# Seven block products in place of eight in the second feed-forward product, with the operand sums on VectorE and GpSimd

## The chip, the cores and the metric

The kernel runs on one core of a Trainium2 chip. The metric is the device time of one launch in microseconds (us): 325.04 us before the change, median of three runs (324.2 to 325.07). All times of "before" below are of runs on the same chip in the same rounds as the kernel they are set against.

## The reference, cut to what matters

Windowed attention (each query sees keys at most 32 positions away), then a two-layer feed-forward block with a tanh gelu between the layers. All inputs are float32.

```python
def reference(q, k, v, w_in, w_out):          # q, k, v: [8, 8, 576, 64]
    s = q @ k.transpose(0, 1, 3, 2) / 8       # only |i - j| <= 32 kept
    attn = softmax(s) @ v
    x = attn.transpose(0, 2, 1, 3).reshape(4608, 512)
    h = x @ w_in                              # w_in  [512, 2048]
    g = 0.5 * h * (1 + tanh(c * (h + 0.044715 * h**3)))
    return g @ w_out                          # w_out [2048, 512]
```

## The kernel before

The 4608 rows are worked in nine tiles of 512 (0 to 8). In each tile TensorE does the first product (16 groups of four 512-column matmuls, each group followed by a gelu on ScalarE), then the second product. The attention of the batch that the next tile needs is woven into the second product. While the first product runs, VectorE casts q and k of that batch to float16, and a DMA transposes them.

```python
PLAN = {3: ([-1], [0]), 14: ([], [1]), 24: ([0], [2]), 35: ([1], [3]), 46: ([2], [4]), 58: ([3], [])}

    def cast_and_turn(b):
        # ... buffers ...
        for src, dst in ((qr, q16), (qt, qt16)):
            for pr in range(NPAIR):
                nc.vector.tensor_copy(...)                 # 4 casts of q, 4 of its tail
            nc.sync.dma_start_transpose(...)
        for pr in range(NPAIR):
            nc.vector.tensor_copy(k16[:, pr, :, :, :], kr[:, :, 2 * pr:2 * pr + 2, :])
            nc.sync.dma_start_transpose(...)               # 4 of k; then its tail

    def ffn_in(t, fc, d0=0, d1=4):
        # ... bank ph; gTs[t] is one single buffer for all tiles ...
        for dc in range(d0, d1):
            nc.tensor.matmul(ph, w_in16[...], xT[...], start=(dc == 0), stop=(dc == 3))
        if d1 == 4:
            nc.scalar.activation(gTs[t][:, fc, :], ph, AF.Gelu_apprx_tanh)

    def ffn_out(t, t4, fc):
        # ... four row blocks t4 of 128, sixteen matmuls of 512 columns each ...
            nc.tensor.matmul(py[:, cols], gTs[t][:, f, t4 * 128:t4 * 128 + 128],
                             w_out16[:, f, cols], start=(f == 0), stop=(f == NF - 1))
        if f == NF - 1:
            yo = yp.tile([128, 512], FP32, name="yo", tag="yo")      # yp has 3 buffers
            # ... copy out of PSUM, store row block t4 at once ...
```

The softmax here doesn't subtract the row's maximum and nothing guards it: scores larger than these inputs give would overflow.

## Time and profile before

| | before |
|---|---|
| time, median | 324.63 us (in the rounds of the change) |
| span of the profiled run | 323.7 us |
| first matmul of tile 1 / 2 / 3 / 7 / 8 | 62.54 / 96.15 / 129.75 / 264.18 / 292.44 us |
| end of the last matmul | 320.12 us |

The chain that ended last, in order of time, gives the period of a tile; its columns are start, length, engine, tile, line and how many instructions. Each line is the start of a first product.

```profile
96.15 0.65 PE mm L439 x3
...
129.75 0.65 PE mm L439 x3
...
163.36 0.65 PE mm L439 x3
```

The period is 33.60 us.

### The profile page before, as it was taken

Reading aid. Unit: us, or ns where it says so; the run is one execution under the profiler, and the core shown is the slowest. Engines: PE = TensorE matmul, PEld = TensorE weight load, DVE = VectorE, ACT = ScalarE, POOL = GpSimd, SP = SyncE. Lnnn points to the kernel's source line nnn. Section 1 sums busy time; section 2 is a strip of 40 time slices with the busy share of each in tenths; the row PEclk is TensorE's granted clock in tenths of the full one; section 3 lists DMA queues with packets and bytes.
Section 4 is the critical chain, followed back from the end, with each engine's and each line's share of the span. In section 5 each row is a group of like instructions: output and inputs, shape, how many; then the busy total and the mean of one; then the engine's idle time right before and its main releaser. Section 6 shows DMA issues by size and latency. Waiting matters only on the chain.

```text
span 323.7 us, 5827 instructions
## 1 busy us (share of the span) xinstructions
PE 311.7 (96%) x2265; PEld 153.4 (47%) x2265; DVE 136.0 (42%) x290; ACT 201.8 (62%) x316; POOL 59.5 (18%) x82
## 2 busy tenths in 40 slices
PE   7688999999999999999999999999999999999995
PEld 2463545444554445444544454445444544444444
DVE  5655587641556064705570467034713530110011
ACT  1757577578667766777577766777668577705600
POOL 3646356292031101300040104010000000000000
PEclk9959999999999999999999999999999999999999
DMA  7999998999989596949495979799270220031022
GB/s 208 259 362 362 381 277 230 251 161 157 248 155 160 95 245 159 169 88 251 115 155 116 221 161 135 134 203 183 75 122 17 67 58 9 0 91 41 0 60 70
DMA packets 120490, 50.57 MB, mean 156 GB/s; under 512 B 100784, under 2 KB 112048, under 8 KB 120464
## 3 DMA queue, kind: packets, MB, share of 16 engines
q1 hardware_dynamic: 88752, 45.07, 58.2%
q0 software_dynamic: 31520, 4.98, 21.0%
q8 instruction: 17, 0.28, 0.4%
q10 hardware_dynamic: 192, 0.16, 0.2%
q14 instruction: 9, 0.07, 0.1%
HBM read 37.62 MB, written 9.44 MB: 145 GB/s over the span
## 4 chain that ended last, share of the span: by engine, by line
PE 93%; SPq 2%; DMA 2%; DVE 1%; ACT 0%; issue 0%; POOL 0%; POOLq 0%
PE mm L461 39%; PE mm L439 24%; PE ph L439 14%; PE ps_o L381 5%; PE ps_s L348 5%; PE ps_d L381 4%; DMA vr<-in_v_dram 2%; SPq L126 1%; PE py L461 1%; ACT gT L443 0%; SPq L135 0%; PE pt L277 0%; DVE w_out L186 0%; PE pt L279 0%; DVE KT L285 0%
## 5 line engine op out<-in xcount | busy, mean ns | idle before, releaser
L461 PE MATMUL mm<-w_out,gT 128*128 128x512 f16 (+1 forms) x576 | 132.0, 377 | 0.8 <-DVE w_out L186 0.8
L439 PE MATMUL mm<-xT,w_in 128*128 128x512 f16 x360 | 89.0, 382 | 0.0
L439 PEld LDWEIGHTS <-w_in 128*128 128x128 f16 x576 | 56.2, 98 | 68.6 <-DVE w_in L186 1.5
L461 PEld LDWEIGHTS <-gT 128*128 128x128 f16 x592 | 54.2, 98 | 61.8 <-issue 0.6
L443 ACT ACTIVATE gT<-mm 128x512 f16<-128x512 f32 x90 | 53.7, 597 | 35.5 <-PE mm L439 35.5
L439 PE MATMUL ph<-xT,w_in 128*128 128x512 f16 x216 | 57.3, 381 | 1.2 <-ACT gT L443 1.2
L354 ACT ACTIVATE pe<-ps_s 128x704 f16<-128x704 f32 x64 | 43.3, 727 | 9.9 <-PE ps_s L348 9.2
L395 ACT ACTIVATE lt<-ps_d 128x480 f32<-128x480 f32 (+3 forms) x40 | 22.2, 555 | 43.2 <-PE ps_d L381 43.1
L443 ACT ACTIVATE gT<-ph 128x512 f16<-128x512 f32 x54 | 32.2, 597 | 13.3 <-PE ph L439 13.3
L405 DVE TENSOR_TENSOR xT<-ps_o,lt 128x480 f16<-128x480 f32 (+5 forms) x38 | 20.3, 552 | 46.9 <-ACT lt L396 46.8
L411 DVE TENSOR_TENSOR xT<-ps_o,lt 128x384 f16<-128x384 f32 (+1 forms) x8 | 4.3, 541 | 80.7 <-ACT lt L396 80.7
L363 DVE TENSOR_TENSOR pe<-pe,mask 128x704 f16<-128x704 f16 x64 | 34.4, 543 | 6.3 <-ACT pe L354 4.0
L465 DVE COPY yo<-mm 128x512 f32<-128x512 f32 x35 | 23.9, 685 | 31.1 <-PE mm L461 28.4
L166 POOL DMA_DIRECT2D V<-in_v_dram x24 | 23.8, 1005 | 63.6 <-PE ps_o L381 47.4
L381 PEld LDWEIGHTS <-V 128*64 128x64 f16 x336 | 18.9, 114 | 18.1 <-issue 11.9
L381 PE MATMUL ps_o<-pe,V 128*64 128x160 f16 (+2 forms) x244 | 22.8, 249 | 1.6 <-POOL V L258 1.5
L396 ACT ACTIVATE lt<-lt 128x480 f32<-128x480 f32 (+3 forms) x40 | 23.5, 588 | 1.3
L381 PE MATMUL ps_d<-pe,ones 128*64 128x192 f16 (+2 forms) x264 | 23.8, 246 | 0.0
L348 PE MATMUL ps_s<-QT,KT 64*128 64x192 f16 (+5 forms) x336 | 19.1, 230 | 2.2 <-DVE KT L285 2.2
L381 PEld LDWEIGHTS <-ones 128*64 128x64 f16 x336 | 19.5, 115 | 0.0
L348 PEld LDWEIGHTS <-KT 64*128 64x128 f16 x336 | 10.9, 95 | 10.6 <-issue 4.2
L168 POOL DMA_DIRECT2D V<-in_v_dram x6 | 5.3, 878 | 56.3 <-PE ps_d L381 39.2
(56 smaller groups left out, 154.3 us busy)
## 6 DMA issues: line engine op xcount, KB each, us to landing
kr<-in_k_dram SPq DMA_DIRECT2D x32, 256.0 KB
qr<-in_q_dram SPq DMA_DIRECT2D x6, 1024.0 KB
V<-in_v_dram POOLq DMA_DIRECT2D x30, 128.0 KB, 5.6
wst<-in_moe_w_in_dram SPq DMA_DIRECT2D x3, 1024.0 KB
wst<-in_moe_w_out_dram SPq DMA_DIRECT2D x3, 1024.0 KB
qr<-in_q_dram SPq DMA_DIRECT2D x8, 256.0 KB
vr<-in_v_dram SPq DMA_DIRECT2D x16, 128.0 KB
out_dram<-yo SPq DMA_DIRECT2D x30, 48.0 KB
```

Source lines behind the costliest of these rows:

```text
L166: nc.gpsimd.dma_start(V[:, c, :, :], v[b, :, 128 * c:128 * c + 128, :].rearrange("h p d -> p h d"))
L348: nc.tensor.matmul(ps[:, h, off:off + 4 * n].rearrange("k (j p) -> k j p", j=4), KTs[b % 2][r0:r0 + 64, pr, k0:k0 + 128], QTs[b][r0:r0 + 6 ...
L354: nc.scalar.activation(pe, ps[:, :, 0:w], AF.Exp, scale=SCALE)
L363: nc.vector.tensor_tensor(pe, pe, m.rearrange("p (o w) -> p o w", o=1).broadcast_to(list(pe.shape)), op=ALU.mult)
L381: nc.tensor.matmul(bk[r0:r0 + 64, at:at + 4 * n].rearrange("d (j p) -> d j p", j=4)[:, :, p0 - q0:p1 - q0], V[:, c, 2 * pr + h, :] if w == ...
L395: nc.scalar.activation(lt[:, 0:n], d[:, 0:n], AF.Ln)
L396: nc.scalar.activation(lt[:, 0:n], lt[:, 0:n], AF.Exp, scale=-1.0)
L405: nc.vector.tensor_tensor(xT[:, g, pos:pos + e], o[:, done:done + e], lt[:, done:done + e], op=ALU.mult)
L439: nc.tensor.matmul(ph, w_in16[:, dc, fc * 128:fc * 128 + 128], xT[:, dc, t * 512 % RING:t * 512 % RING + 512], start=(dc == 0), stop=(dc = ...
L443: nc.scalar.activation(gTs[t][:, fc, :], ph, AF.Gelu_apprx_tanh)
L461: nc.tensor.matmul(py[:, cols], gTs[t][:, f, t4 * 128:t4 * 128 + 128], w_out16[:, f, cols], start=(f == 0), stop=(f == NF - 1))
L465: (nc.scalar.copy if last and half == 0 else nc.vector.tensor_copy)(yo[:, cols], py[:, cols])
```

## The change

The second product of tiles 1 to 8 is cut into 2 by 2 blocks and done with seven block products instead of eight, by sums of blocks made beforehand (the scheme known as Winograd's form of Strassen's). T1 to T4 are sums of weight blocks, made once, at the end of tile 0. S1 to S4 are sums of gelu blocks, made in every tile, a quarter at a time after every fourth gelu; the groups of the first product are taken in another order, so that each quarter has its blocks together. The products of a pair are accumulated in PSUM (the memory that this kernel's matmuls write their results to, in pieces called banks) where the scheme allows it; VectorE adds the rest when it empties a bank. TensorE's share should shrink by an eighth. The price is work on VectorE and GpSimd, and outputs that are finished later.

```diff
+WINO = [("A11", "B11", True), ("S2", "T2", True), ("A12", "B21", False), ("S3", "T3", False),
+        ("S1", "T1", True), ("A22", "T4", False), ("S4", "B22", False)]
+PLAN = {6: "s0 v-1", 24: "s1", 26: "m0", 32: "x-1", 40: "m1", ...}
-    yp = ctx.enter_context(tc.tile_pool(name="yp", bufs=3))
+    yp = ctx.enter_context(tc.tile_pool(name="yp", bufs=2))
 ...
     def ffn_in(t, n, d0=0, d1=4):
 ...
             nc.scalar.activation(gTs[t][:, fc, :], ph, AF.Gelu_apprx_tanh)
+            if t and n % 4 == 3:
+                sums(t, n // 4)
+    def combine_w():
+        for eng, dst, x, y in ((nc.vector, T1, B12, B11), (nc.vector, T2, B22, T1),
+                               (nc.gpsimd, T3, B22, B12), (nc.gpsimd, T4, B21, T2)):
+            eng.tensor_tensor(dst, x, y, op=ALU.subtract)
+    def sums(t, i):
+        third = nc.vector if t == 1 else nc.gpsimd
+        for eng, dst, x, y, op in ((nc.vector, S1, A21, A22, ALU.add),
+                                   (nc.vector, S2, S1, A11, ALU.subtract),
+                                   (third, S3, A11, A21, ALU.subtract),
+                                   (nc.gpsimd, S4, A12, S2, ALU.subtract)):
+            eng.tensor_tensor(dst, x, y, op=op)
 ...
+    def ffn_out(t, i):                       # 7 products of 16 matmuls of 256 columns
+        n, blk, f = i // 16, i // 8 % 2, i % 8
 ...
+        elif n == 5:
+            nc.vector.tensor_tensor(C21, py, M1, op=ALU.add)
+            for x in range(2):
+                store(t, 2 + x, yo[:, 2 + x, :])
+                if end:                      # last tile
+                    store(t, x, yo[:, x, :], left)
+    def ffn_last(t):
+        for x in range(2):
+            nc.vector.tensor_tensor(yo[:, x, right], py[:, x, :], yo[:, x, right], op=ALU.add)
+            store(t, x, yo[:, x, :], right if t == NT - 1 else slice(0, 512))
 ...
         if t == 0:
             load_v(2)
+            combine_w()
```

Tile 0 keeps its eight products. Its output copies share the buffers `yp`, now two.

More of the change, by code (lines that the diff above doesn't have):

```diff
@@ L35, in width @@
     return sum(4 * (p1 - p0) for (_, _, p0, p1) in pieces)
-PLAN = {3: ([-1], [0]), 14: ([], [1]), 24: ([0], [2]), 35: ([1], [3]), 46: ([2], [4]), 58: ([3], [])}
+WINO = [("A11", "B11", True), ("S2", "T2", True), ("A12", "B21", False), ("S3", "T3", False),
+        ("S1", "T1", True), ("A22", "T4", False), ("S4", "B22", False)]
+PLAN = {6: "s0 v-1", 24: "s1", 26: "m0", 32: "x-1", 40: "m1", 42: "v0 s2", 48: "x0", 56: "m2",
+        61: "v1 s3", 64: "x1", 80: "m3", 81: "v2 s4", 88: "x2", 97: "v3", 104: "m4", 112: "x3"}
 TURN_0 = {9: 0, 11: 1, 13: 2, 15: 3}
@@ L49 @@
            [(t4, fc) for t4 in (2, 3) for fc in range(16)])
-END = (3, 0, 2, 1)
 RING = 1536
@@ L413, in spread, with ffn_in @@
                 lt[:, 0:n].rearrange("d (r q) -> d r q", r=NPAIR), op=ALU.mult)
-    def values(b, g):
-        o, d = weigh(b, g)
-        spread(b, g, o, invert(b, g, d))
     gTs = {}
     phs = {}
-    def ffn_in(t, fc, d0=0, d1=4):
-        if fc == 0 and d0 == 0:
+    def ffn_in(t, n, d0=0, d1=4):
+        fc = n // 2 + 8 * (n % 2) if t else n
+        if n == 0 and d0 == 0:
             gTs[t] = gp.tile([128, NF, 512], FP16, name="gT", tag="gT")
@@ L432, in ffn_in @@
                 if t:
-                    i = (0, 2, 1)[fc % 3] if fc < NF - 1 else 2
+                    i = (first(t), 2, 1 - first(t))[n % 3] if n < NF - 1 else 2
                 else:
@@ L443, in ffn_in, with first @@
             nc.scalar.activation(gTs[t][:, fc, :], ph, AF.Gelu_apprx_tanh)
+            if t and n % 4 == 3:
+                sums(t, n // 4)
+    def first(t):
+        return (t + 1) % 2
+    wino = {}
+    def combine_w():
+        t12 = stage.tile([128, 2, 8, 256], FP16, name="t12", tag="stage")
+        t34 = stage.tile([128, 2, 8, 256], FP16, name="t34", tag="stage")
+        B11, B12, B21, B22 = (w_out16[:, r:r + 8, c:c + 256] for r in (0, 8) for c in (0, 256))
+        T1, T2, T3, T4 = t12[:, 0], t12[:, 1], t34[:, 0], t34[:, 1]
+        for eng, dst, x, y in ((nc.vector, T1, B12, B11), (nc.vector, T2, B22, T1),
+                               (nc.gpsimd, T3, B22, B12), (nc.gpsimd, T4, B21, T2)):
+            eng.tensor_tensor(dst, x, y, op=ALU.subtract)
+        s12 = stage.tile([128, 2, 8, 256], FP16, name="s12", tag="stage")
+        s34 = stage.tile([128, 2, 8, 256], FP16, name="s34", tag="stage")
+        yo = stage.tile([128, 4, 512], FP32, name="y4", tag="stage")
+        wino.update(B11=B11, B21=B21, B22=B22, T1=T1, T2=T2, T3=T3, T4=T4, S1=s12[:, 0],
+                    S2=s12[:, 1], S3=s34[:, 0], S4=s34[:, 1], yo=yo)
@@ new lines, in sums @@
+    def sums(t, i):
+        g, r = gTs[t], slice(2 * i, 2 * i + 2)
+        A11, A21, A12, A22 = (g[:, r0 + 2 * i:r0 + 2 * i + 2, c:c + 256]
+                              for r0 in (0, 8) for c in (0, 256))
+        S1, S2, S3, S4 = (wino[f"S{n}"][:, r, :] for n in (1, 2, 3, 4))
+        third = nc.vector if t == 1 else nc.gpsimd
[4 more added lines that the diff above has]
+            eng.tensor_tensor(dst, x, y, op=op)
@@ L445 @@
     out_v = out.rearrange("(b p j) f -> b j p f", b=B, j=4)
     pys = {}
-    def ffn_out(t, t4, fc):
-        last = t == NT - 1 and t4 == END[-1]
-        if last:
-            half, fc = divmod(2 * fc, NF)
-            halves = [slice(256 * half, 256 * half + 256)] * 2
-        else:
-            half, halves = 0, [slice(0, 512)]
-        for f, cols in enumerate(halves, fc):
-            if f == 0:
-                pys[t4] = bank((END.index(t4) if t == NT - 1 else t4) % 2) if half == 0 else \
-                    psO.tile([128, 512], FP32, name="py2", tag="O")
-            py = pys[t4]
-            nc.tensor.matmul(py[:, cols], gTs[t][:, f, t4 * 128:t4 * 128 + 128],
-                             w_out16[:, f, cols], start=(f == 0), stop=(f == NF - 1))
-        if f == NF - 1:
-            yo = yp.tile([128, 512], FP32, name="yo", tag="yo")
-            (nc.scalar.copy if last and half == 0 else nc.vector.tensor_copy)(
-                yo[:, cols], py[:, cols])
-            m = 0
-            while m < 128:
-                b, c = divmod(t * 512 + t4 * 128 + m, S)
-                q0, n = (0, cut(b)) if c < 4 * cut(b) else (cut(b), 144 - cut(b))
-                j, p = divmod(c - 4 * q0, n)
-                e = min(n - p, 128 - m)
-                eng = nc.scalar if last and m else nc.sync if t else nc.gpsimd
-                eng.dma_start(out_v[b, j, q0 + p:q0 + p + e, cols], yo[m:m + e, cols])
-                m += e
@@ new lines, in store, with ffn_out_0 @@
+    def store(t, t4, yo, cols=slice(0, 512), eng=None):
+        m = 0
+        while m < 128:
+            b, c = divmod(t * 512 + t4 * 128 + m, S)
+            q0, n = (0, cut(b)) if c < 4 * cut(b) else (cut(b), 144 - cut(b))
+            j, p = divmod(c - 4 * q0, n)
+            e = min(n - p, 128 - m)
+            (eng or nc.sync).dma_start(out_v[b, j, q0 + p:q0 + p + e, cols], yo[m:m + e, cols])
+            m += e
+    def ffn_out_0(t4, fc):
+        if fc == 0:
+            pys[t4] = bank(t4 % 2)
+        nc.tensor.matmul(pys[t4], gTs[0][:, fc, t4 * 128:t4 * 128 + 128], w_out16[:, fc, :],
+                         start=(fc == 0), stop=(fc == NF - 1))
+        if fc == NF - 1:
+            yo = yp.tile([128, 512], FP32, name="yo", tag="yo")
+            nc.vector.tensor_copy(yo, pys[t4])
+            store(0, t4, yo, eng=nc.gpsimd)
@@ new lines, in ffn_out @@
+    def ffn_out(t, i):
+        n, blk, f = i // 16, i // 8 % 2, i % 8
+        a, w, new = WINO[n]
+        if i % 16 == 0 and new:
+            pys[n % 2] = bank((first(t) + n) % 2)
+        py = pys[n % 2].rearrange("p (b c) -> p b c", b=2)
+        if a[0] == "A":
+            r0, c0 = 8 * (int(a[2]) - 1) + f, 256 * (int(a[1]) - 1) + 128 * blk
+            lhsT = gTs[t][:, r0, c0:c0 + 128]
+        else:
+            lhsT = wino[a][:, f, 128 * blk:128 * blk + 128]
+        nc.tensor.matmul(py[:, blk, :], lhsT, wino[w][:, f, :], start=(new and i % 16 == 0),
+                         stop=(i % 16 == 15), skip_group_check=True)
+        if i % 16 < 15:
+            return
+        yo, left, right = wino["yo"], slice(0, 256), slice(256, 512)
+        C11, C12, C21, C22 = (yo[:, r:r + 2, c] for r in (0, 2) for c in (left, right))
+        end = t == NT - 1
+        M1, U2, U3 = C21, C12, C22
+        if n == 0:
+            nc.vector.tensor_copy(M1, py)
+        elif n == 1:
+            nc.vector.tensor_tensor(U2, py, M1, op=ALU.add)
+        elif n == 2:
+            nc.vector.tensor_copy(C11, py)
+        elif n == 3:
+            nc.vector.tensor_tensor(U3, py, M1, op=ALU.add)
+        elif n == 4:
+            nc.vector.tensor_tensor(C22, py, U3, op=ALU.add)
+        elif n == 5:
[4 more added lines that the diff above has]
+                    store(t, x, yo[:, x, :], left)
@@ L478 @@
+    def ffn_last(t):
+        py = pys[0].rearrange("p (b c) -> p b c", b=2)
+        yo, right = wino["yo"], slice(256, 512)
+        for x in range(2):
+            nc.vector.tensor_tensor(yo[:, x, right], py[:, x, :], yo[:, x, right], op=ALU.add)
+            store(t, x, yo[:, x, :], right if t == NT - 1 else slice(0, 512))
     cast_open(0)
@@ L588 @@
                 ffn_in(t, fc)
-        plan = PLAN if att else {3: ([-1], [])} if t == B - 1 else {}
+        plan = PLAN_0 if not t else PLAN if att else {6: "v-1", 32: "x-1"} if t == B - 1 else {}
         def group(g):
@@ L597 @@
             load_qk(b + 1)
-        if t == 0:
-            ods = {}
-        for i in range(64):
-            for act in PLAN_0.get(i, "").split() if t == 0 else ():
+        ods = {}
+        for i in range(113 if t else 65):
+            for act in plan.get(i, "").split():
                 kind, g = act[0], int(act[1:])
@@ L623 @@
                     ods[g] = (o, invert(bb, gg, d))
+                    if t and g < 0 and b + 1 < B:
+                        load_v(b + 1)
                 else:
                     spread(*group(g), *ods[g])
-            if t and i in plan:
-                for g in plan[i][0]:
-                    values(*group(g))
-                    if g < 0 and b + 1 < B:
-                        load_v(b + 1)
-                for g in plan[i][1]:
-                    score(*group(g))
-                    mask(*group(g))
-            if t:
-                ffn_out(t, END[i // NF] if t == NT - 1 else i // NF, i % NF)
-            else:
-                ffn_out(t, *ORDER_0[i])
+            if t == 0 and i < 64:
+                ffn_out_0(*ORDER_0[i])
+            elif t and i < 112:
+                ffn_out(t, i)
         if t == 0:
             load_v(2)
+            combine_w()
+        else:
+            ffn_last(t)
         begun = 2 if att else 0
```

## The prediction

> **What bounds the kernel now.** I read the page's busy shares first, then the chain that ended last, then the groups by shape, then the timeline at the places where the change puts new waits. The page:
>
> ```profile
> PE 311.7 (96%) x2265; PEld 153.4 (47%) x2265; DVE 136.0 (42%) x290; ACT 201.8 (62%) x316; POOL 59.5 (18%) x82
> PE 93%; SPq 2%; DMA 2%; DVE 1%; ACT 0%; issue 0%; POOL 0%; POOLq 0%
> ```
>
> TensorE is busy for 96% of the span and carries 93% of the chain: every microsecond taken from its stream counts, unless something makes it wait. What the second product costs, and what a 256-column matmul costs, stands in the chain by time (start, length, what) in tiles 7 and 8:
>
> ```profile
> 279.17 13.27 PE mm L461 x61
> 292.44 0.86 PE mm L439 x4
> ...
> 306.25 12.11 PE mm L461 x64
> 318.36 1.76 PE py L461 x16
> ```
>
> Four matmuls of 512 columns take 0.86 us, 0.216 each (the 61 above them, with a few records missing from the trace, 0.2175). The row of 64 mixes 48 of 512 with 16 of 256 columns: 48 x 0.216 leaves 0.109 for a short one. The last row is the one that matters: 16 matmuls of 256 columns, each with its own weight load, took 0.110 us each.
>
> Two places off TensorE. First, VectorE against GpSimd, from narrow cuts of the timeline (start, length, engine, line):
>
> ```profile
> 29.39 0.43 DVE L186 CAST w_in<-wst 128x512 f16<-128x512 f32 x1 [1.55 <-DMA wst<-in_moe_w_in_dram]
> 29.42 0.87 POOL L186 CAST w_in<-wst 128x512 f16<-128x512 f32 x1 [1.11 <-DMA wst<-in_moe_w_in_dram]
> ...
> 29.73 0.84 DVE L186 CAST w_in<-wst 128x512 f16<-128x512 f32 x1
> ...
> 43.54 0.62 POOL L186 CAST w_out<-wst 128x512 f16<-128x512 f32 x1 [1.37 <-DMA wst<-in_moe_w_out_dram]
> 43.65 0.88 DVE L363 TENSOR_TENSOR pe<-pe,mask 128x704 f16<-128x704 f16 x1 [0.54 <-ACT pe L354]
> ```
>
> The first to start keeps its own length (0.43 cast, 0.62 GpSimd cast); the second is stretched (0.62 to 0.87, 0.43 to 0.84, and the mask product from its 0.56 to 0.88). They take turns, whole instruction by whole instruction. Second, stores and their buffers, from the timeline, the list of DMA issues about 56 us (size, us from issue to landing) and the list of the store's instructions about 311 us (ns, first and last start):
>
> ```profile
> 55.79 1.28 POOL L474 DMA_DIRECT2D out_dram<-yo  x2
> ...
> 57.71 0.69 DVE L465 COPY yo<-mm 128x512 f32<-128x512 f32 x1
> ```
>
> ```profile
> out_dram<-yo POOLq DMA_DIRECT2D x2, 256.0 KB, 4.9
> ```
>
> ```profile
> L474 SPq DMA_DIRECT2D out_dram<-yo x5: 328/364/380, 310.5 to 312.1; - x5
> ```
>
> A store from GpSimd's queue in tile 0 lands 4.9 us after issue; the third tile copy starts at 57.71, before that, because there are three buffers. And SyncE issues one store per (312.1 - 310.5)/4 = 0.4 us.
>
> **What the Trainium skill says.** "TensorE: Matmul & The Clock Gate", Back-to-back issue gap: 262 cycles at 2.4 GHz for 256 columns, 109 ns. The trace has 110; it agrees. "SBUF — State Buffer", SBUF: two separate sides: VectorE and GpSimd share one port pair, an exclusive lock held for the whole instruction, and a VectorE instruction with two SBUF inputs is in it. The pairs above agree. "GPSIMD Engine Reference", 3.1: a two-input addition of 2048 fp32 elements takes 4497 ns on GpSimd, about 2.2 ns per element. This trace has no two-input GpSimd operation, so its length for f16 is my largest unknown.
>
> **The change part by part.**
> 1. TensorE. Per tile 64 x 0.216 = 13.82 us become 7 x 16 = 112 matmuls of 256 columns, 112 x 0.110 = 12.32. Gain 1.50 us a tile, 12.0 us for eight (tile 8 had 32 short ones already: 13.89, the same within 0.1). All of it lies on the chain. This assumes the weight load of each stays hidden, as in the row of 16.
> 2. Sums of gelu outputs. Four times per tile, after every fourth gelu: S1, S2 on VectorE, S3, S4 on GpSimd (in tile 1 S3 on VectorE). VectorE: the mask products (704 and 640 elements: 558 and 524 ns in the groups by shape) give some 0.45 us for 512, so 3.6 us a tile. GpSimd: estimate from the skill's page 512 x 2.1 ns + 0.18 = 1.25 us, 10 us a tile. VectorE's seven additions or copies out of PSUM are 7 x 0.69 = 4.8 us in place of 4 x 0.685 = 2.7. Tiles 2 to 6 have VectorE busy 4.2 + 10.8 = 15.0 of 33.6 us, GpSimd some 5; both have room. Taking turns, the last S2 of a tile comes some 2.2 us after the last gelu (one GpSimd sum, then S1 and S2, with one turn lost). TensorE needs it at matmul 22 of the second product: 22 x 0.110 = 2.4 us, plus the score and value matmuls put in before (0.55 + 0.53), so some 3.5 us after the first product, against gelu's 0.8 + 2.2. Tiles 2 to 6: nothing. Tiles 7 and 8 have no or fewer insertions: 0.3 us in all.
> 3. Tile 1. Here the sums of weights must be made too: T1, T2 on VectorE (2048 elements, 1.2 us each) and T3, T4 on GpSimd, by the page 4.5 us each. GpSimd first issues the last store and five loads of V, which ended at 70.7 in the timeline of before; so T3 and T4 hold the port from some 72 to 81, while VectorE has twelve sums left, gets one in between, and needs 11 x 0.4 plus three turns of GpSimd after that. The last S2 then comes at 87 to 88; TensorE asks for it at 81.5. Cost 6 us; if GpSimd does f16 at 1.5 ns per element, 2 us.
> 4. Tile 0. The tile buffers of its outputs go from three to two. The third copy (57.71) must now wait for the first store's landing, 55.79 + 4.9 = 60.7. VectorE is in order; behind it are the copies of the turned tails (0.69 + 0.28 + 0.41 later: 61.97), which the last scores need at 60.58. TensorE waits 1.4 us.
> 5. The end. Before, the last store is issued 0.5 us after the last matmul, from two queues, and the span ends 3.6 us after that matmul (320.12 to 323.7). Now rows 2 and 3 and the left halves of rows 0 and 1 can be stored only after the sixth product, 1.76 us before the end, plus 0.7 for the addition: 1.05 us before the last matmul's end. I count 11 stores there and 4 after the last addition, all from SyncE: the fifteenth starts 14 x 0.4 = 5.6 us after the first, so 4.5 us after the last matmul instead of 0.5. Cost 4.0 us.
> Sum: -12.0 + 0.3 + 6 + 1.4 + 4.0 = -0.3 us, with fast GpSimd sums -4.3 us; with no collision at all -6.6.
>
> **The rivals.** (A) The gain arrives whole: the port does not bind in tile 1, and the parts in 4 and 5 are all: 325 - 6.6 = 318.4. For it: the twelve sums need under 6 us of VectorE, which idles 10 us there; whoever wrote it moved S3 to VectorE in tile 1 alone, so looked at this place. Against: the stretched pairs. (B) The port binds in every tile: were a GpSimd sum 1.5 us rather than 1.25, S2 and S4 would slip past TensorE's need, some 1 us in each of tiles 2 to 6: 330. For it: ten microseconds of GpSimd in a first product of 14, beside VectorE's thirteen casts. Against: the slack of about a microsecond at matmul 22, and S3 and S4 are wanted only in products 4 and 7. (C) The matmuls do not hold 0.110, because 47% of weight-load busy becomes more: 98 ns per load against 110 per matmul is close. At 0.125 the product costs 14.0 and nothing is gained: 325 + 12 = 337. Against: 32 in a row in tile 8 held 0.110. (D) VectorE's evictions hold up the two PSUM banks: a bank is asked for again one product, 1.76 us, later, and its reader takes 0.69 but stands behind masks and spreads of some 1.7 us; I expect waits under 0.3 us a tile.
>
> **Range and chances.** I put 60% on the port in tile 1 with 2 to 7 us, 25% on A, 15% on B, C or worse. Between my sum (324.7) and A (318.4), weighted, the point is 322.0. Eight in ten: 316 to 328. Faster by over 2% means below 318.5, which A reaches by a hair and only if the end or tile 0 costs less than I count: 0.22. Slower (above 331.5) needs B or C: 0.06. Within 2%: 0.72.
>
> **What would show it.** The group of short matmuls: 896 of them at 0.110 start to start, and the chain's stretches without pause in tiles 2 to 6 shortened from 33.6 to 32.1 us a tile (wrong if the period does not shrink). Tile 1: GpSimd's two long sums at 4 to 5 us, VectorE's sums idle or stretched beside them, and TensorE waiting at the second block product for a sum; if TensorE runs through, 3 is wrong. Tile 0: the third copy waiting for a store's landing and TensorE for the tail copies, 1.4 us. The end: 15 stores 0.4 us apart and over 7 us from the last matmul to the end. If GpSimd's sum of 512 takes under 0.8 us, A holds and the time is about 318; if the gap at the end is under 5 us, I have overcounted there.

## More of the kernel before

ScalarE needs two tables of functions: gelu in the first product, exp and log in the second.

Nothing in this kernel reads gelu outputs except TensorE. The table of gelu is not loaded by the program: the builder puts the load in ahead of the first gelu of each tile.

In tile 1 the four casts of q take 1.48 us in all (timeline: start, length, engine, line, operation, how many):

```profile
63.19 1.48 DVE L305 CAST q<-qr 128x512 f16<-128x512 f32 x4
```

The busy times in a cut of tile 1 (bounds, us, then busy us and count for PE, PEld, DVE, ACT and POOL, the clock granted to TensorE, share and GB/s of the DMA):

```profile
82.00:87.00 5.00, 5.00 (x49) 2.52 (x49) 2.85 (x8) 2.47 (x5) 0.00 (x0) 1.00 1.35 255
```

TensorE has no pause here and a full clock.

The timeline at the start of tile 3 shows the load of the gelu table (start, length, engine, line, operation):

```profile
129.62 1.28 ACT L443 ACT_TABLE_LOAD   x1
...
131.30 0.60 ACT L443 ACTIVATE gT<-mm 128x512 f16<-128x512 f32 x1 [0.40 <-PE mm L439]
```

The load begins as soon as ScalarE is free, at the same moment as the tile's first matmul, and lies beside the first matmuls. The first gelu then waits 0.40 us for TensorE: the table costs nothing.

## The result, and the profile after

The changed kernel took 336.27 us, median of four runs (334.7 to 338.01), beside 324.63 us. The ratio is 1.036 (95% interval 1.0302 to 1.0418): it is slower. Ratios in this document are the mean time of one kernel's fast runs over that of the other's of the same rounds, so they are not quite the ratio of the medians quoted.

The page of the changed kernel, busy shares and chain by engine:

```profile
PE 301.2 (90%) x2633; PEld 190.0 (57%) x2633; DVE 204.2 (61%) x392; ACT 199.9 (60%) x315; POOL 136.3 (41%) x144
...
PE 66%; DMA 9%; SPq 8%; DVE 8%; ACT 4%; issue 2%; POOL 0%; DVEq 0%; ACTq 0%; POOLq 0%
```

TensorE does less (301.2 us for 311.7), but its share of the chain fell from 93% to 66%. Something else now sets the time in many places. The chain by time, at the starts of tiles 2 and 3 and in the last second product:

```profile
104.99 0.65 PE mm L440 x3
...
138.21 0.65 PE mm L440 x3
...
313.21 12.24 PE mm L517 x112
```

The last line is the predicted saving: 112 short matmuls in 12.24 us, 0.109 each. The starts divide the span. The last column of the table gives the prediction's own terms (the 1.50 us of part 1 taken off in each tile, and its costs added):

| stretch, us | before | after | difference | in the prediction's sum |
|---|---|---|---|---|
| to the start of tile 1 | 62.54 | 62.99 | +0.45 | +1.4 |
| tile 1 | 33.61 | 42.00 | +8.39 | +4.5 |
| tiles 2 to 6 together | 168.03 | 166.18 | -1.85 | -7.5 |
| tile 7 | 28.26 | 27.77 | -0.49 | -1.35 |
| tile 8, to the last matmul's end | 27.68 | 26.51 | -1.17 | -1.35 |
| last matmul to the end | 3.58 | 7.55 | +3.97 | +4.0 |
| sum | 323.7 | 333.0 | +9.3 | -0.3 |

Two rows carry the miss of 9.6 us: tiles 2 to 6 (5.65) and tile 1 (3.9). The profiled run (334.7 us) is the fastest of the four; the median lies 1.6 us above it, and experiment 5 comes back to that.

**Tiles 2 to 6.** In tile 3 the second product took 18.31 us (153.13 to 171.44) where it took 19.80 before (143.56 to 163.36): a gain of 1.49 for the predicted 1.50. But the first product took 14.92 us (138.21 to 153.13) for 13.81 (129.75 to 143.56): 1.11 us are lost in a part that the change does not seem to touch. The timeline of the changed kernel there:

```profile
139.81 1.28 ACT L444 ACT_TABLE_LOAD   x1 [2.09 <-PE mm L440]
141.10 0.60 ACT L444 ACTIVATE gT<-mm 128x512 f16<-128x512 f32 x1
...
141.75 1.02 PE L440 MATMUL mm<-xT,w_in 128*128 128x512 f16 x4 [0.94 <-ACT gT L444]
```

Read the brackets: the table load itself waited 2.09 us for a matmul. Before, it waited for nothing. So its 1.28 us now lie after the first matmuls instead of beside them, the first gelu comes late, and TensorE, which has three banks for this product, stands 0.94 us for the bank that the gelu should have emptied. The waits by line have it in seven tiles (engine, line, what it waited for: us in total, times, longest; the longest is tile 8, before which ScalarE had long been idle):

```profile
ACT L444 <- PE mm L440: 23.3, 7, 10.8
```

**Tile 1.** Narrow cuts of the timeline:

```profile
66.53 10.85 DVE L308 CAST q<-qr 128x512 f16<-128x512 f32 x1
68.96 4.12 POOL L462 TENSOR_TENSOR t<-w_out 128x2048 f16<-128x2048 f16 x1
72.98 4.11 POOL L462 TENSOR_TENSOR t<-w_out,t 128x2048 f16<-128x2048 f16 x1
...
84.44 0.74 PE L351 MATMUL ps_s<-QT,KT 64*128 64x160 f16 x8 [7.00 <-DMA KT<-k]
```

One cast of q, 0.41 us elsewhere, took 10.85: it spans GpSimd's loads of V (its first 2.4 us lie beside these alone) and both weight sums, T3 and T4, and ends 0.3 us after the second. Eleven casts of q, its tail and k are behind it, then the transposes, then the scores. TensorE waits 7.00 us for the transposed k. The chain says the same (q casts of one kind merged):

```profile
66.08 11.97 DVE q L308 x4
...
81.96 2.44 DMA KT<-k
84.44 0.74 PE ps_s L351 x6
85.97 3.95 PE mm L517 x18
```

The last line shows a second cost: 18 short matmuls took 3.95 us, not 18 x 0.109 = 1.96. After seven idle microseconds the clock is down:

```profile
82.00:87.00 5.00, 2.56 (x30) 1.87 (x31) 4.93 (x8) 2.00 (x4) 3.23 (x3) 0.50 0.43 85
```

The granted clock is 0.50 where it was 1.00 before. Wait (7.0) and slow matmuls (2.0) make 9.0 of the 9.9 us by which tile 1 lost (8.39, and the 1.50 that the product should have gained).

**The sums of gelu outputs**, by group (busy us, mean ns):

```profile
L480 POOL TENSOR_TENSOR s<-gT 128x512 f16<-128x512 f16 x28 | 34.7, 1241 | 111.0 <-ACT gT L444 110.7
...
L480 DVE TENSOR_TENSOR s<-gT 128x512 f16<-128x512 f16 x36 | 31.7, 887 | 48.6 <-ACT gT L444 48.5
...
L480 DVE TENSOR_TENSOR s<-s,gT 128x512 f16<-128x512 f16 x32 | 13.6, 426 | 3.8 <-DVE s L480 0.9
```

A GpSimd sum of 512 takes 1.24 us. VectorE's first sum (S1; the group also holds the four S3 of tile 1) shows 887 ns where S2, of the same size, shows 426. In the timeline of tile 3 each S1 lies beside S3 of its own quarter, which GpSimd began before it (S3 from 146.49 to 147.65, S1 from 146.89 to 147.93): one GpSimd sum first, as predicted. In tiles 2 to 8 TensorE never waits for these sums.

**Tile 0.** The third copy and the scores behind it:

```profile
59.74 0.69 DVE L502 COPY yo<-mm 128x512 f32<-128x512 f32 x1 [3.89 <-DMA out_dram<-yo]
...
61.01 0.35 PE L351 MATMUL ps_s<-QT,KT 64*128 64x96 f16 x8 [2.30 <-DVE QT L274]
```

The copy waits for a store's landing and TensorE for the copies behind it, 2.30 us. The table shows only +0.45 up to tile 1 because this execution had reached that place at 58.72, where the one before reached its scores at 60.58 without a pause.

**The end**, from the list of store instructions (first, median and largest ns; first and last start):

```profile
L492 SPq DMA_DIRECT2D out_dram<-y x15: 286/363/421, 324.4 to 330.2; - x15
```

Fifteen stores over 5.8 us, 0.41 apart, the last 4.75 us after the last matmul (325.45).

### The profile page after: what moved, and what is told of

Read it like the earlier page. It is cut to its first block, busy times and chain, and to the rows that moved or that the text cites. A ratio compares the mean times of both kernels' runs of the same rounds, so it can differ in the third digit from the quotient of the medians.

```text
span 333.0 us, 6772 instructions
## 1 busy us (share of the span) xinstructions
PE 301.2 (90%) x2633; PEld 190.0 (57%) x2633; DVE 204.2 (61%) x392; ACT 199.9 (60%) x315; POOL 136.3 (41%) x144
## 4 chain that ended last, share of the span: by engine, by line
PE 66%; DMA 9%; SPq 8%; DVE 8%; ACT 4%; issue 2%; POOL 0%; DVEq 0%; ACTq 0%; POOLq 0%
PE mm L517 29%; PE mm L440 17%; PE ph L440 10%; SPq L138 4%; PE ps_o L384 4%; PE ps_s L351 4%; DVE q L308 4%; DMA wst<-in_moe_w_in_dram 3%; ACT L444 3%; PE ps_d L384 3%; DMA qr<-in_q_dram 2%; DMA out_dram<-yo 2%; SPq L129 1%; ACT gT L444 1%; DVE y L529 1%
## 5 line engine op out<-in xcount | busy, mean ns | idle before, releaser
L480 POOL TENSOR_TENSOR s<-gT 128x512 f16<-128x512 f16 x28 | 34.7, 1241 | 111.0 <-ACT gT L444 110.7
L480 DVE TENSOR_TENSOR s<-gT 128x512 f16<-128x512 f16 x36 | 31.7, 887 | 48.6 <-ACT gT L444 48.5
L517 PEld LDWEIGHTS <-s 128*128 128x128 f16 x512 | 49.0, 99 | 8.0 <-issue 0.2
L480 POOL TENSOR_TENSOR s<-gT,s 128x512 f16<-128x512 f16 x32 | 37.1, 1159 | 35.0 <-DVE s L480 30.3
L517 PE MATMUL mm<-t,s 128*128 128x256 f16 x384 | 47.5, 276 | 0.0
L517 PEld LDWEIGHTS <-gT 128*128 128x128 f16 x384 | 36.5, 99 | 7.8
L517 PE MATMUL mm<-w_out,gT 128*128 128x256 f16 x256 | 33.9, 279 | 0.0
L366 DVE TENSOR_TENSOR pe<-pe,mask 128x704 f16<-128x704 f16 x64 | 32.3, 539 | 1.9 <-ACT pe L357 1.6
```

The source lines that it names most:

```text
L366: nc.vector.tensor_tensor(pe, pe, m.rearrange("p (o w) -> p o w", o=1).broadcast_to(list(pe.shape)), op=ALU.mult)
L480: eng.tensor_tensor(dst, x, y, op=op)
L517: nc.tensor.matmul(py[:, blk, :], lhsT, wino[w][:, f, :], start=(new and i % 16 == 0), stop=(i % 16 == 15), skip_group_check=True)
```

## The experiments

Twelve kernels ran; all gave correct results. Their diffs are against the changed kernel unless another is named. "Before" is 324.1 to 327.1 us in all of them. The changed kernel itself was timed in the first rounds only (336.27 us), so what an experiment saves is a difference between medians of different rounds, and of chips that need not be the same; "before" moved by 0.7 us between the rounds of the result and of experiments 1 to 8 (324.63, 324.61, 325.27). The runs of experiments 9 to 12 are single ones, of unknown state, and were made for their traces. Theory at this point: (a) the table load inherits a wait; (b) GpSimd's weight sums starve the casts of tile 1; (c) the stores at the end and (d) the two tile buffers cost what parts 5 and 4 say. Rival for the middle tiles: the sums, by whatever way, slow the first product (B of the prediction). Rival for tile 1: it is only the length of one GpSimd instruction, so that short ones would do no harm.

**1. Load the gelu table by hand**, before the next tile's first matmuls. The sums stay as they are.

```diff
+        if t and plan:
+            load_gelu_table()
         begun = 2 if att else 0
```

> The changed kernel with the load of the gelu table issued as an instruction of its own, ahead of the first product's first matmuls, in tiles 1 to 7. Theory (the load now sits behind the first gelu's wait for TensorE, because that gelu has two waits since GpSimd reads the same tile, and costs 1.1 us in each of tiles 2 to 7 and 0.5 in tile 8): 7 us less than the changed kernel, about 329 us, and the periods of tiles 2 to 6 fall from 33.2 to 32.1 us. Rival (the first gelu waits for GpSimd's last sum of the tile before, or for TensorE itself; the table is only drawn into the same wait): no change, 336 us.

Measured: 329.78 us (328.55 to 330.85), ratio 1.0161 (1.0119 to 1.0202). The starts of tiles 2 to 7 are 32.12 us apart (105.89, 138.01, 170.13, ...); 33.22 without the load. At the start of tile 4:

```profile
169.65 1.28 ACT L88 ACT_TABLE_LOAD   x1
...
171.73 0.60 ACT L450 ACTIVATE gT<-mm 128x512 f16<-128x512 f32 x1 [0.80 <-PE mm L446]
```

The load has no wait again. 6.5 us are back, and the period is the predicted 32.1. So the whole loss of the middle tiles was the place of this load; the sums, which are still there, cost nothing. How it came about: the buffer of the gelu outputs is now also read by GpSimd, so a tile's first gelu has one more wait than before. In the instruction list of the built program this gelu of tiles 2 to 8 waits for GpSimd, its wait for TensorE has become an instruction of its own, and the automatic load stands between the two. In the kernel before, the wait for TensorE is on the gelu itself, behind the load.

**2. Weight sums T3 and T4 on VectorE.**

```diff
-                               (nc.gpsimd, T3, B22, B12), (nc.gpsimd, T4, B21, T2)):
+                               (nc.vector, T3, B22, B12), (nc.vector, T4, B21, T2)):
```

> The changed kernel with all four sums of weights on VectorE. Theory (in tile 1 GpSimd's two long sums keep the shared port from VectorE's casts, and so delay the transposes and the scores): 8 to 9 us less, about 327.5 us; tile 1 takes 33 to 34 us instead of 42. Rival (the transposes or the loads of q and k are late by themselves in tile 1, or the twelve sums of gelu outputs are what is late): VectorE has 2.4 us more to do, so the same 336 us or 2 us more.

Measured: 327.22 us (325.54 to 328.41), ratio 1.0079 (1.0031 to 1.0127): 9.05 us less. The four casts of q together took 1.89 us. Tile 1 took 32.75 us instead of 42.00. Theory b holds for where the time went: GpSimd's two instructions were nearly the whole cost of tile 1 (9.25 of the 9.9 us). VectorE does each in 1.2 us.

**3. The same sums on GpSimd, each in four instructions of 512.** If VectorE gets a turn between two instructions, this is a cure.

```diff
-            eng.tensor_tensor(dst, x, y, op=ALU.subtract)
+            step = 2 if eng is nc.gpsimd else 8
+            for r in range(0, 8, step):
+                eng.tensor_tensor(dst[:, r:r + step], x[:, r:r + step], y[:, r:r + step],
+                                  op=ALU.subtract)
```

> The changed kernel with GpSimd's two sums of weights cut into four instructions each of 512 elements per partition: the same work on GpSimd, about 1.15 us a piece. If the two engines take turns instruction by instruction (my prediction's model), VectorE gets a cast between any two pieces, the slowest q cast takes 1.5 us instead of 10.9, and most of the 8 to 9 us of tile 1 come back: 329 to 331 us. Rival (back-to-back GpSimd instructions keep the port, as it kept it over three loads of V and both long sums): one cast lasts some 10 us again and the time stays at 336 us.

Measured: 336.65 us (335.41 to 337.15), ratio 1.0379 (1.0339 to 1.0419): no gain. The timeline:

```profile
67.34 12.30 DVE L308 CAST q<-qr 128x512 f16<-128x512 f32 x4
...
70.22 4.52 POOL L464 TENSOR_TENSOR t<-w_out 128x512 f16<-128x512 f16 x4
...
74.68 4.68 POOL L464 TENSOR_TENSOR t<-w_out,t 128x512 f16<-128x512 f16 x4
```

The casts got nothing between the pieces: one lasted 8.80 us, up to the last piece. So the length of one GpSimd instruction is not the cause, and the prediction's "they take turns" is not a general rule. Experiments 7 and 9 to 12 are about this.

**4. Stores of the last tile spread out**: each part as soon as it is finished, the last ones from two queues.

```diff
             nc.vector.tensor_copy(C11, py)
+            if end:
+                for x in range(2):
+                    store(t, x, yo[:, x, :], left)
 ...                                   # likewise C22; rows 2, 3 left and the last right
+                    store(t, x, yo[:, x, :], right, (nc.sync, nc.scalar)[x])
```

> The changed kernel with the last tile's stores issued as soon as each quarter is done (left halves of rows 0 and 1 after the third product, right halves of rows 2 and 3 after the fifth) and the last eleven shared between two queues. Theory (fifteen stores at 0.4 us from one queue set the end): from last matmul to the end 4.5 to 5 us instead of 7.55, so 3 us less, about 333.3 us. Rival (the end waits for the memory traffic of 1 MB, not for the issuing): under 1 us less.

Measured: 333.05 us (331.35 to 333.81), ratio 1.0255 (1.0213 to 1.0298). From the last matmul (324.89) to the end 4.7 us instead of 7.55. Theory c holds; which share the earlier issue has and which the second queue, this one run does not separate.

**5. Three tile buffers again.**

```diff
-    yp = ctx.enter_context(tc.tile_pool(name="yp", bufs=2))
+    yp = ctx.enter_context(tc.tile_pool(name="yp", bufs=3))
```

> The changed kernel with three tile buffers for tile 0's outputs, as before the change. Theory (the third copy waits 3.9 us for a store to land, TensorE waits 2.3 us for the tail copies behind it, and in some executions the clock falls to 0.5 to 0.6 for some 4 us after that wait): 2 to 3 us less than the changed kernel, about 333.5 us, and less spread between runs. Rival (tile 0's wait is hidden, because the prologue's loads decide when tile 1 starts): 336 us.

Measured: 332.3 us (331.73 to 332.89), ratio 1.0216 (1.018 to 1.0252): 4.0 us less, more than the wait of 2.3 us in the trace. Two things fit. The spread of the times fell from 3.3 to 1.2 us. And the kept profiles show what such a wait can bring with it. With two buffers TensorE waits at this place in all ten (1.45 to 3.81 us). In five of them (experiments 2, 3, 7, 9 and 11) the granted clock then is 0.50 for some 3.4 us (read in cuts of half a microsecond; half of that, 1.7 us, is my estimate of the time lost); in the other five (the changed kernel, 1, 4, 10 and 12) it stays at 1.00. With three buffers (5, 6 and 8) there is neither the wait nor the fall. The length of the wait alone does not decide: one of 2.09 us had the fall, one of 3.12 us had not. So this wait costs the clock in some executions. That it did so in the timed runs of the changed kernel is argued, not shown: its one profile is of its fastest run, and has no fall.

**6. All four together** (1, 2, 4, 5).

> All four repairs together: table load of its own, weights' sums on VectorE, early stores at the end, three buffers. Theory (four separate costs that add up): 336.3 - 6.5 - 9 - 3.2 - 2.3 = 315.3 us, 3% faster than the kernel before; tiles 1 to 6 at 32.1 to 32.5 us each. Rival (they overlap, or the block products cost something that none of the four names): 318 to 321 us.

Measured over five rounds: 314.52 us (313.83 to 315.63), ratio 0.9667 (0.9634 to 0.97). The four gave 6.5 + 9.05 + 3.2 + 4.0 = 22.8 us singly, and 336.27 - 314.52 = 21.75 together: they are separate costs, within the noise of such differences, and account for the result. (By the ratios to "before" of the same rounds, times 324.63 us: 6.5, 9.1, 3.4 and 4.7, 23.7 in all, and 22.5 together.) The change itself is good for 10 to 11 us once they are gone.

**7. Weight sums after the casts**, T1 and T2 on VectorE, T3 and T4 on GpSimd, so that no cast is in their way.

```diff
+        wino["todo"] = ((nc.vector, T1, B12, B11), (nc.vector, T2, B22, T1),
+                        (nc.gpsimd, T3, T2, B11), (nc.gpsimd, T4, B21, T2))
 ...
+            if t == 1:                          # after cast_and_turn
+                for eng, dst, x, y in wino["todo"]:
+                    eng.tensor_tensor(dst, x, y, op=ALU.subtract)
```

> The changed kernel with tile 1's sums of weights put behind VectorE's casts: T1 and T2 follow the casts on VectorE, and T3 (as T2 - B11) and T4 are still on GpSimd and need T2, so they can only meet VectorE's sums of gelu outputs, as I had predicted it. Theory (a VectorE sum with two SBUF inputs is kept waiting too for as long as GpSimd runs back to back): the transposes are in time, but the last S2 is late: TensorE waits 4 to 7 us in tile 1's second product, 331 to 334 us. Rival (only VectorE's casts are kept waiting, sums are not): tile 1 takes 33 to 34 us, 327.5 us.

Measured: 334.97 us (334.26 to 335.21), ratio 1.0294 (1.0258 to 1.033), just above the expected range. The transposes were in time, but the gelu sums of VectorE were starved instead:

```profile
73.56 4.16 DVE L479 TENSOR_TENSOR s<-s,gT 128x512 f16<-128x512 f16 x1
...
77.64 5.57 DVE L479 TENSOR_TENSOR s<-gT 128x512 f16<-128x512 f16 x2
```

TensorE then waited three times, 1.63, 1.70 and 1.69 us, for such sums, and the clock was 0.50 between 88 and 92 us. So moving the casts away does not cure it: two GpSimd instructions of 4 us in this tile held up the VectorE sums that lay beside them as they had held up the casts.

**8. Experiment 6, with the last spread of the attention one step earlier** (step 31 for 32 in the plan). The chain of the changed kernel has some 0.25 us per tile in which value matmuls wait for it.

```diff
-PLAN = {6: "s0 v-1", 24: "s1", 26: "m0", 32: "x-1", 40: "m1", ...
+PLAN = {6: "s0 v-1", 24: "s1", 26: "m0", 31: "x-1", 40: "m1", ...
```

> As the run with all four repairs, and the spread of the fifth group is queued on VectorE ahead of the second product's addition instead of behind it (one step earlier in the plan). Theory (the first value matmuls wait 0.25 us for that spread in tiles 1 to 6): 1 to 1.5 us less than all four alone, 314 us. Rival (the addition then holds up the bank instead, or the next step waits): no difference.

Measured over five rounds: 312.57 us (311.7 to 314.76), ratio 0.9616 (0.958 to 0.9651), 3.8% faster than before and the best version here. It is 1.95 us less than experiment 6, a little more than the theory asked for; in the profiles the mean period of tiles 2 to 6 fell from 32.13 to 31.87 us, the 0.25 us a tile that it named. The ranges of the timed runs overlap. Its page:

```profile
PE 297.9 (96%) x2633; PEld 188.4 (61%) x2633; DVE 203.8 (66%) x394; ACT 200.5 (64%) x315; POOL 130.3 (42%) x142
```

TensorE is back at 96%, of a shorter span.

**9. Twelve plain copies on GpSimd in place of its weight sums** (from experiment 2, so the sums themselves are on VectorE). Is it the second input that keeps VectorE out?

```diff
+        for k in range(12):
+            r, dst = k % 4 * 2, (s12[:, 1], s34[:, 0], s34[:, 1])[k // 4]
+            nc.gpsimd.tensor_copy(dst[:, r:r + 2, :], w_out16[:, r:r + 2, 0:256])
```

> The changed kernel with all sums of weights on VectorE, and on GpSimd, where the two long sums stood, twelve one-input copies of 512 elements back to back, whose results are overwritten later (the output stays right). In the kernel before, back-to-back GpSimd casts and VectorE casts of the prologue took turns; in tile 1 eight back-to-back sums gave none. If any back-to-back GpSimd work keeps the port, VectorE's q casts, which start near 68.5 us, again end only with the copies: one lasts 5 us or more, and the time is about 332 us. If only GpSimd instructions with two inputs keep it, the casts take turns with the copies, none lasts over 1.2 us, and the time is 327 to 329 us.

Measured: 334.42 us in one run beside 324.12. The timeline:

```profile
69.76 6.60 DVE L308 CAST q<-qr 128x512 f16<-128x512 f32 x1
...
69.92 6.91 POOL L467 COPY s<-w_out 128x512 f16<-128x512 f16 x12
```

One-input copies of 0.58 us do it too: one cast lasted 6.60 us, eleven copies long.

**10 and 11. Seven GpSimd copies beside the casts, with pauses and without.** Both from experiment 2, with the gelu sums of tile 1's first three quarters put behind the copies. In 10 each copy reads the newest gelu output and must wait for it; in 11 it reads weights that are long there.

```diff
+            if t == 1 and 5 <= n <= 11:
+                nc.gpsimd.tensor_copy(wino["S4"][:, 6:8, :],
+                                      gTs[1][:, fc, :]...)      # 11: w_out16[:, n, :]
```

> The kernel with all weight sums on VectorE, with seven GpSimd copies of 512 put into tile 1 beside the q, turned-tail and k casts; each copy reads the newest gelu output, so each must wait some 0.3 us for the next gelu (one every 0.86 us, a copy takes 0.57). The sums of gelu outputs of this tile's first three quarters come after the copies, so a wait of TensorE for them is not the question; the length of the casts is. If VectorE gets the port as soon as GpSimd pauses: no cast lasts over 1.1 us, and all thirteen casts (4.7 us without GpSimd's work) are done within 7 us of the first. If any work of GpSimd there starves VectorE: one cast of 3 us or more.

> The same kernel but the seven copies read weights, which are long there, so that they run back to back for about 4 us. If a back-to-back run keeps the port: one cast lasts 3 us or more, for nearly as long as the run. If VectorE gets a turn between two instructions whatever the gap: no cast over 1.1 us, as with the pauses.

Measured: with pauses the four q casts took 2.71 us, the longest cast 0.83 us, all thirteen were done 6.97 us after the first began. The times (329.64 and 332.66 us in one run each) were not the question. Without pauses:

```profile
71.91 2.70 DVE L308 CAST q<-qr 128x512 f16<-128x512 f32 x4
...
72.07 5.25 POOL L446 COPY s<-w_out 128x512 f16<-128x512 f16 x7
```

The four q casts took 2.70 us here as well. This contradicts the theory that I had taken from experiments 3 and 9: back-to-back copies do take turns here. Two things differ between 9 and 11: in 9 the copies read pieces of 256 columns, in 11 whole rows; and in 9 they write to twelve places, in 11 all to one. Copies to one place must wait for each other; the listing of the compiled program has a wait for GpSimd itself on each of the seven, and on only two of the twelve. The seven of experiment 10 have it too, so that run says nothing of pauses by itself.

**12. Experiment 9 with one place for all twelve copies.** Nothing else is changed.

```diff
-            nc.gpsimd.tensor_copy(dst[:, r:r + 2, :], w_out16[:, r:r + 2, 0:256])
+            nc.gpsimd.tensor_copy(s34[:, 1, 6:8, :], w_out16[:, r:r + 2, 0:256])
```

> The twelve GpSimd copies of the run with copies, same sources, same place in the program, but all written to the same slice, so that each has to wait for the completion of the one before it; nothing else is changed. If such a wait is what lets VectorE in (the seven copies that took turns had it, the twelve that did not take turns had it on two only): no cast of q over 1.1 us, the four done within 3.5 us. If it is the form of the operands (the twelve read 256-column pieces, the seven whole rows): one cast lasts 5 us or more again.

Measured (332.88 us in one run):

```profile
69.27 2.70 DVE L308 CAST q<-qr 128x512 f16<-128x512 f32 x4
69.43 11.01 POOL L467 COPY s<-w_out 128x512 f16<-128x512 f16 x12
```

The four casts took 2.70 us (the longest 0.82), where one alone had lasted 6.60. Between 9 and 12 only the place written to differs, and with it the wait. Where a GpSimd copy had to wait for the end of the one before it, VectorE got in between; where it had not, GpSimd went on and VectorE stayed out until the run of copies was nearly over.

What stays open: whether a like rule holds the other way round. Later in this run one GpSimd copy took 2.70 us beside VectorE's casts of k, which have no wait on each other; but the casts of q and its tail have none either, and GpSimd got in between them. Also, in the prologue (what runs ahead of tile 0) of the kernel before, VectorE got in between two GpSimd casts of which the second has no wait, and in experiments 3 and 9 it got in ahead of the last instruction of the run, but in the changed kernel not between T3 and T4. And in the changed kernel the cast was held for 2.4 us beside GpSimd's loads of V, before any sum. Why a run sometimes lets VectorE in before its last instruction, these runs do not say.

## Why the prediction was wrong

The prediction said 322.0 us and within 2%; it was 336.27 us and slower. By its own parts:

1. TensorE, gain 1.50 us a tile: right. 112 short matmuls took 12.24 us, and with the table load put right the period went from 33.60 to 32.12 us, the number that the prediction asked for.
2. The sums, "Tiles 2 to 6: nothing": **this step failed**, though not in what it worked out. The sums are as long as estimated (1.24 us for 1.25), and TensorE does not wait for them in the second product. (The 15.0 us of VectorE and some 5 of GpSimd that it calls room are the load before the change; after it, tile 3 has 21.4 and 14.0 of 33.2 us, still room.) What was missing is that a new reader of the gelu buffer on another engine gives the tile's first gelu one more wait, and that the automatic table load then stands behind that gelu's wait for TensorE, which costs TensorE 1.1 us a tile. Experiment 1 gave back 6.5 us. Rival B named nearly that size for these tiles (1 us each), for a wait that is not there; the number came close for a wrong reason.
3. Tile 1, "6 us": **the second failed step**, of the right mechanism. The port does bind, but the text let VectorE get "one in between", expected the casts to be done by then, and so looked for the wait at the last gelu sum. In fact one cast was held from 66.53, before T3 began, until after T4, and the casts feed the transposes and scores, which TensorE wants earlier. The term measured 9.9 us instead of 6 (8.39 and the unrealised 1.50), of which the lowered clock is about 2.0, a term that the prediction did not have. Experiment 2 confirms it (9.05 us). "They take turns, whole instruction by whole instruction" was read from pairs in the prologue; experiments 3 and 9, against 11 and 12, show that a run of independent GpSimd instructions gave no such turn until its last one.
4. Tile 0, 1.4 us: right in mechanism and place. TensorE's wait was 2.30 us, and undoing it gave 4.0 us: mis-sized, and the clock that five of ten profiles lost after the wait was no term of it.
5. The end, 4.0 us: right, 3.97 us; 15 stores, 0.41 us apart.

Rivals: A did not happen; only with the weight sums on VectorE and the other three repairs (experiment 6) does the gain arrive nearly whole. C (short matmuls slower than 0.110) and D (evictions holding banks) did not come in: 0.109 us each, and the second product of tile 3 gained its full 1.49 us. The chance of 0.06 for slower was too small mostly because the list of rivals went through the new instructions and their engines, and not through what the new readers add to old instructions.

## What to carry to other kernels

When a change gives a buffer a new reader on another engine, look at what now waits in front of the next writer of that buffer, and at any automatic table load there; a load placed by hand kept 1.1 us a tile off the path. Don't put a run of independent GpSimd instructions beside VectorE work that heads a chain to TensorE: either give the few long operations to VectorE, or make each GpSimd instruction depend on the one before (the second is shown for the length of the casts only, in experiments 11 and 12; it was not tried on the weight sums, and those runs, single ones with extra copies, do not tell its worth in time). And after a change that trades TensorE time for work elsewhere, take the losses one by one before judging it: this one went from 3.6% slower to 3.8% faster with the same seven block products.

## What the Trainium skill lacked or had wrong

- "SBUF — State Buffer", "SBUF: two separate sides": the lock is told as held for one instruction, won by whoever starts first. The runs show that twelve independent GpSimd copies of 0.58 us kept a VectorE cast out for 6.60 us, and that the same copies with a wait on each other let each cast end within 0.82 us. The page should say what happens from one instruction to the next.
- "TensorE: Matmul & The Clock Gate", "What's actually happening": the clock is said to fall after an idle window of about 3.4 us. Here it fell to 0.50 after a wait of 7.00 us, which agrees, but also, for some 3.4 us, after single waits of 2.09 to 2.83 us in four profiles, while it stayed at 1.00 after one of 3.12 us; and to 0.50 after three waits of 1.63 to 1.70 us with short work between them.
- "GPSIMD Engine Reference", 3.1: only a float32 length for a two-input operation (4497 ns for 2048). In float16 2048 took 4.12 us and 512 took 1.16 to 1.24 us, so the narrower type hardly helps.
- No page that I found says that an automatic table load can carry a wait of the activation behind it. It cost 1.1 us per tile here, 6.5 us in all.
